# First keys projected ahead of the sketch's turn, third group's factors ahead of turns that wait for loads

## The chip, the cores and the metric

The kernel runs on one core of a Trainium2 chip. The metric is device time in microseconds, the median of several executions; lower is better.

## The reference

Polynomial-sketch attention on 4 batches of 4 heads, 1088 rows of 32, followed by a two-layer network on the rows:

```python
def phi(x):                       # S1, S2: 8 x 32
    a = einsum('rd,bhsd->bhsr', S1, x)
    b = einsum('rd,bhsd->bhsr', S2, x)
    return einsum('bhsi,bhsj->bhsij', a, b).reshape(*x.shape[:-1], 64)

q_p, k_p = phi(q), phi(k)
kv = einsum('bhsf,bhsd->bhfd', k_p, v)
z = sum(k_p, axis=2)
num = einsum('bhsf,bhfd->bhsd', q_p, kv)
den = einsum('bhsf,bhf->bhs', q_p, z)[..., None] + 1e-06
x = (num / den).transpose(0, 2, 1, 3).reshape(4352, 128)
h = x @ w_in                      # 128 x 2048
out = (h - tanh(h)) @ w_out       # 2048 x 128
```

## The kernel before

The 4352 rows are cut into eleven groups (`GROUPS`) of 256 to 512 rows; group 0 to 2 belong to batch 0, group 3 begins batch 1, and group 5 holds the end of batch 1 and the beginning of batch 2. Each batch first needs its keys. Each group needs the factors of its queries, then the numerators, then the rows x, then 16 blocks of the first layer with tanh on ACT, and 16 of the second.

**The planner.** Every instruction, or short run of instructions, is an operation with an engine, an expected cost in ns, a priority and its data dependences (`Program.op`). `Program.listed` places the operations by a list schedule over the expected costs, `schedule` takes the best of six passes, and each engine then carries out its operations in exactly that order. `Program.line(tags)` adds an order between named operations: each comes after the one named before it, also across engines. The change is in such lines alone, so no operation is added or removed by it; the planner runs again on the new order, and the place of every other operation can change with it.

**Names used below.** b is a batch, g a group.
- `pS` (L499), `wkm` (L502), `pSel` (L515), `s2m` (L518): the sketch matrices, turned by PE and masked by DVE. `pSel` writes the PSUM bank that `wkm` reads, so it waits for `wkm`.
- `kTb0`, `kTb1` (L537): DVE's turns of the two parts of a batch's k. `kp00`, `kp01` (L544): PE's projections of the keys of batch 0, in two halves; the other batches have one. `kabb` (L555): DVE's turn of these. `kpsb` (L561): a copy to PSUM. `wkb0`, `wkb2` (L570): products of key factors on DVE; the rest (`wk03` and so on) are made by POOL. `gramb` (L581, PE), `gmb` (L588, DVE), `foldb` (L593, PE), `ub` (L596, DVE): from the key factors to a weight that the queries of the batch need for their denominators.
- `sumsb` (L609), `kvzb` (L617), `turnb` (L620), `ndwb` (L623): the sums over a batch's keys.
- `qTg` (L631): DVE's turn of a group's q. `pg` (L653, PE), `qqg` (L682), `aug` (L685), `dng` (L688, all DVE), `dsg` (L697, PE), `rdg` (L700), `ang` (L704, DVE): factors and the reciprocal denominators. `qpg0`, `qpg1` (L716): products, on DVE and POOL for groups 0, 1 and the first of a batch, on POOL alone for the others. `qpTg0`, `qpTg1` (L723): DVE's turns of these.
- `wg` (L669, PE): the numerators. `xg` (L731): the rows, copied by ACT for groups 0 and 1, by DVE for the others.
- `hg_j` (L792, PE) and `tg_j` (L795, ACT): a block of the first layer and its tanh, over three PSUM banks in turn. L805: the second layer, summed in one bank. The linear part h @ w_out is taken together as one 128x128 matrix (`wtx`, `wcx`, `wp`; its two halves at L772, L773) and added at L784. L812 turns the finished rows into `osb`, and L818 issues the stores.
- L483 and L494 are matmuls on zeros with which the planner fills idle time of PE early in the kernel.

**The loads.** Batch 0 is loaded by ACT's and SP's queues at the start. `lk1`, the first load of batch 1, waits for `qpT01`; v and q of batch 1 follow it in SP's queue. The loads of batch 2 wait for `x2` and those of batch 3 for `x4`; the stores at L818 share this queue.

**The order written by hand.** DVE's first 33 operations stand in one line (L911 to L913). In it `s2m` comes before `kab0`, `qT0` before `kps0`, and after `qpT11` come `kT10` and `kT11`. The factors of group 2 (`qq2` to `an2`) and `qT3` are in no line. PE's first operations stand in the line of L919, with `pSel` right after `pS`.

Of the kernel before, what the change touches and what calls it, by code (L numbers as in the profile page):

```python
# [307 lines left out]
def bass_polysketch_attn__then__act_tanh_shrink_kernel(nc, q, k, v, S1, S2, moe_w_in, moe_w_out, out):  # L308
    P = Program(nc)

    def sb(name, shape, dtype=F32):
        return nc.alloc_sbuf_tensor(name, shape, dtype).ap()
# [21 lines left out]
    s2m = sb("s2m", [128, H, D])  # L334
    wkm = sb("wkm", [128, 2, R, 2])
# [7 lines left out]
    wk = sb("wk", [128, 9, 4, 64])  # L343
# [34 lines left out]
    b = c = at = 0  # L378
    for n0, n1 in GROUPS:
        parts = [(b, c, n0)]  # L380
        c += n0
        if n1:
            assert n1 == n0
            b, c = b + 1, n1
# [3 lines left out]
        if c == CB:  # L388
            b, c = b + 1, 0
# [481 lines left out]
    for g in range(NG):  # L871
# [35 lines left out]
        if g:  # L907
            layers(g)
    P.tags["lq1"].deps.add(P.tags["kT00"])
    P.tags["lk1"].deps.add(P.tags["qpT01"])  # L910
    P.line(["kT00", "wkm", "kT01", "s2m", "kab0", "qT0", "kps0", "gm0", "wk00", "u0", "wk02", "qq0", "au0", "dn0", "qT1",  # L911
            "rd0", "an0_1", "an0_0", "qp00", "qpT00", "qpT01", "qq1", "au1", "dn1", "qT2",
            "rd1", "an1_1", "an1_0", "qp10", "qpT10", "qpT11", "kT10", "kT11"])  # L913
    for g in range(4, NG):
        P.line([f"x{g - 2}", f"qT{g}"])
    for b in range(2, B):
        P.line([f"x{first[b] - 2}", f"kT{b}0", f"kT{b}1"])
    P.line(["x1", "kT10"])
    P.line(["pS", "pSel", "kp00", "kp01", "gram0", "fold0", "p0", "sums00", "ds0", "sums01", "turn0", "p1", "w0"])  # L919
    P.line(["w0", "h0_2", "ds1", "wt0", "w1", "p2"])  # L920
    P.line(["kvz0", "cin0", "ndw0", "cin1", "x0", "t0_0"])
    P.line(["t0_2", "cin2"])
# [32 lines left out]
```

## Time and profile before

| | before |
|---|---|
| median of 3 runs | 108.63 us (107.75 to 108.82) |
| profiled execution | 109.61 us |
| its span | 107.8 us |
| PE busy | 102.2 us (95%), 1287 matmuls |
| ACT busy | 80.5 us (75%) |
| DVE busy | 65.4 us (61%) |
| POOL busy | 33.3 us (31%) |
| granted clock of TensorE | 1.0 |

The span is the part of one execution that the profiler covers; the execution's own time has some 1.8 us around it. In a timeline a row gives its start, its length, the engine, the line of the code, the operation, the tiles, and, in brackets, how long the engine was idle before and what ended that. Instructions of one engine can overlap by the latency of the pipeline, so the distance from one start to the next is often shorter than the length of a row. The ends of matmuls are modelled.

### The profile page before, as it was taken

The page shows a single profiled execution, that of the slowest core. Times are in us where ns is not written, and L with a number is a line of the kernel's source. Part 1 is how long each engine was busy: PE and PEld are TensorE (multiplying, and loading weights), DVE is VectorE, ACT ScalarE, POOL GpSimd, SP SyncE. Part 2 cuts the span into 40 slices and gives each one's busy share as a digit, 9 for nine tenths or more (in the row PEclk, how much of TensorE's full clock was granted, in tenths as well). Part 3 has the DMA queues.
Part 4 walks back from the last instruction along what each step waited for, and adds up shares of the span by engine and source line. Part 5 has one row for each costly group of instructions (what it writes and reads, how often), then busy time and mean ns, then how long its engine had stood idle before and what let it go on. Part 6 is the DMA issues. An engine that isn't in the chain of part 4 may idle for free.

```text
span 107.8 us, 3131 instructions
## 1 busy us (share of the span) xinstructions
PE 102.2 (95%) x1287; PEld 54.0 (50%) x1287; DVE 65.4 (61%) x164; ACT 80.5 (75%) x193; POOL 33.3 (31%) x59
## 2 busy tenths in 40 slices
PE   6999999997899999999999999999999999999990
PEld 4524656582437444535645534454664634545580
DVE  3556987636971859966379359687366657234030
ACT  0004459999476976897797998798698899999960
POOL 6549437006550300781120420088030060030000
PEclk9999999999999999999999999999999999999999
DMA  2998999800089405005895104000410502203223
GB/s 61 323 275 232 368 252 274 233 17 0 9 258 235 178 5 85 0 6 84 274 290 114 23 0 73 6 3 7 72 25 0 91 0 33 43 0 48 43 44 78
DMA packets 23678, 11.21 MB, mean 104 GB/s; under 512 B 17648, under 2 KB 22384, under 8 KB 23664
## 3 DMA queue, kind: packets, MB, share of 16 engines
q1 hardware_dynamic: 20144, 7.44, 29.8%
q10 hardware_dynamic: 3520, 3.57, 11.0%
q8 instruction: 10, 0.16, 0.7%
q14 instruction: 4, 0.03, 0.1%
HBM read 8.78 MB, written 2.23 MB: 102 GB/s over the span
## 4 chain that ended last, share of the span: by engine, by line
PE 64%; DMA 11%; DVE 7%; SPq 7%; ACT 5%; POOL 2%; issue 1%
PE ps L792 21%; PE ps L805 19%; DMA qraw<-in_q_dram 11%; PE ps L483 6%; ACT tt L795 5%; SPq L434 5%; PE ps L669 3%; PE ps L784 3%; PE ps L653 3%; PE ps L544 2%; PE ps L609 2%; PE ps L830 2%; SPq L818 2%; POOL qp L716 2%; DVE qT L631 2%; DVE qpT L723 1%
## 5 line engine op out<-in xcount | busy, mean ns | idle before, releaser
L795 ACT ACTIVATE tt<-ps 128x448 bf16<-128x448 f32 (+3 forms) x176 | 73.9, 525 | 9.5 <-PE ps L792 8.8
L792 PE MATMUL ps<-xT,w_in 128*128 128x448 bf16 (+3 forms) x176 | 56.6, 334 | 0.3
L805 PE MATMUL ps<-tt,w_out 128*128 128x448 bf16 (+3 forms) x160 | 49.9, 336 | 0.0
L792 PEld LDWEIGHTS ps<-xT,w_in 128*128 128x128 bf16 x176 | 16.8, 97 | 23.8 <-ACT tt L795 14.1
L716 POOL TENSOR_TENSOR qp<-an,qq 128x384 f32<-128x384 f32 (+3 forms) x17 | 14.5, 855 | 41.7 <-DVE an L704 40.9
L805 PEld LDWEIGHTS ps<-tt,w_out 128*128 128x128 bf16 x160 | 16.4, 103 | 7.8
L570 POOL TENSOR_TENSOR wk<-kab 128x256 f32<-128x256 f32 (+1 forms) x18 | 12.6, 700 | 17.7 <-DVE kab L555 16.6
L723 DVE STREAM_TRANSPOSE qpT<-qp 128x448 f32<-128x448 f32 (+3 forms) x22 | 12.4, 581 | 5.4 <-POOL qp L716 5.2
L812 DVE STREAM_TRANSPOSE osb<-ps 128x448 f32<-128x448 f32 (+3 forms) x10 | 6.0, 602 | 8.3 <-PE ps L792 4.1
L700 DVE RECIPROCAL ps<-ps 128x28 f32<-128x28 f32 (+3 forms) x11 | 3.4, 313 | 11.0 <-PE ps L697 11.0
L483 PE MATMUL ps<-wz 128*128 128x256 bf16 (+1 forms) x27 | 8.0, 437 | 1.1 <-DVE hmask L460 1.1
L631 DVE STREAM_TRANSPOSE qT<-qraw 128x256 f32<-128x256 f32 (+2 forms) x12 | 6.4, 530 | 3.1 <-DMA qraw<-in_q_dram 3.1
L682 DVE STREAM_TRANSPOSE qq<-ps 128x448 f32<-128x448 f32 (+3 forms) x11 | 6.4, 577 | 2.4 <-PE ps L653 2.3
L617 ACT ACT_TABLE_LOAD x1 | 1.3, 1283 | 8.5 <-DVE ps L561 8.5
L669 PE MATMUL ps<-qpT,ndw 64*32 64x224 f32 (+3 forms) x176 | 6.2, 339 | 0.9 <-DVE qpT L723 0.9
L537 DVE STREAM_TRANSPOSE kT<-kraw 128x576 f32<-128x576 f32 (+1 forms) x8 | 5.6, 721 | 1.1 <-DMA kraw<-in_k_dram 1.1
L731 DVE CAST xT<-ps 128x384 bf16<-128x384 f32 (+3 forms) x9 | 5.5, 606 | 1.1 <-PE ps L669 0.9
L653 PE MATMUL ps<-qT,wq 64*32 64x224 f32 (+3 forms) x176 | 6.1, 334 | 0.0
L570 DVE TENSOR_TENSOR wk<-kab,ps 128x512 f32<-128x512 f32 (+1 forms) x8 | 5.1, 645 | 0.0
L609 PE MATMUL ps<-wk,vx 128*32 128x64 f32 x288 | 5.1, 221 | 0.0
L609 PEld LDWEIGHTS ps<-wk,vx 128*32 128x32 f32 x288 | 4.2, 110 | 1.4 <-issue 1.3
L483 PEld LDWEIGHTS ps<-wz 128*128 128x128 bf16 x27 | 3.0, 130 | 3.7 <-issue 1.7
(74 smaller groups left out, 82.6 us busy)
## 6 DMA issues: line engine op xcount, KB each, us to landing
kraw<-in_k_dram SPq DMA_DIRECT2D x3, 544.0 KB, 4.5
qraw<-in_q_dram SPq DMA_DIRECT2D x3, 544.0 KB, 6.4
vx<-in_v_dram SPq DMA_DIRECT2D x10, 144.0 KB, 4.1
w_in_f<-in_moe_w_in_dram ACTq DMA_DIRECT2D x2, 512.0 KB, 7.5
w_out_f<-in_moe_w_out_dram ACTq DMA_DIRECT2D x2, 512.0 KB, 8.5
out_dram<-osb SPq DMA_DIRECT2D x16, 56.0 KB, 1.9
out_dram<-osb SPq DMA_DIRECT2D x16, 48.0 KB, 1.8
vx<-in_v_dram SPq DMA_DIRECT2D x4, 112.0 KB, 5.0
```

The source lines that it names most:

```text
L483: P.op("tensor", 213 if x < 16 else 221, lambda e, n=1 if x < 16 else 2: e.matmul(ps[:, 3, 0:256 * n], wz[:, 0:128], wz[:, None, :].to_bro ...
L570: P.op(eng, (dve if eng == "vector" else pool)(64 * n), lambda e: e.tensor_tensor(out=wk[:, t0:t1, :, :].rearrange("p t h (i j) -> p (t h) ...
L609: ins = e.matmul(ps[32 * h:32 * h + 32, sbk, 0:64], vx[i][:, h, t, :], wk[:, t, h, :], start=(t == 0), stop=(t == 8), tile_position=(0, 32 ...
L631: P.op("vector", dve(hi - lo), lambda e, i=b % 2, lo=lo, hi=hi: e.transpose(out=qT[i][:, lo:hi], in_=qraw[i][:, lo:hi]), r=[("qraw", b % 2 ...
L653: ins = e.matmul(o, wq[64 * r:64 * r + 64, b, y, :, :].rearrange("p h x -> p (h x)"), src, start=True, stop=True, tile_position=(64 * r, 3 ...
L669: ins = e.matmul(ps[32 * h:32 * h + 32, 2 + u, 0:32 * nh], ndw[i][64 * u:64 * u + 64, 32 * h:32 * h + 32], src[64 * u:64 * u + 64, h // 2, ...
L682: P.op("vector", dve(16 * n), lambda e: e.transpose(out=a[:, 0:n, :].rearrange("p (r m) x -> p r (m x)", r=2), in_=ps[:, pb[0]:pb[1] + 1:p ...
L716: P.op("vector" if dv else "gpsimd", (dve if dv else pool)(32 * m), lambda e, lo=lo, dv=dv: e.tensor_tensor(out=qp[u][:, lo:lo + m, :].rea ...
L723: P.op("vector", dve(32 * m), lambda e, lo=lo: e.transpose(out=qpT[u][:, 32 * lo:32 * (lo + m)], in_=qp[u][:, lo:lo + m, :].rearrange("p n ...
L792: P.op("tensor", pe(n), lambda e, jb=jb, bk=bk: e.matmul(bk[:, 0:n], w_in[:, 128 * jb:128 * jb + 128], xT[:, t0:t0 + n], start=True, stop= ...
L795: P.op("scalar", act(n), lambda e, ts=ts, bk=bk: e.activation(out=tt[:, ts, 0:n], in_=bk[:, 0:n], func=AF.Tanh, scale=-1.0), r=[kb], w=[(" ...
L805: P.op("tensor", pe(n), lambda e, jb=jb, ts=ts: e.matmul(acc[:, 0:n], w_out[:, jb, :], tt[:, ts, 0:n], start=(jb == 0 and not g), stop=(jb ...
```

## The change

The diff changes the lines of order and nothing else:

```diff
-    P.line(["kT00", "wkm", "kT01", "s2m", "kab0", "qT0", "kps0", "gm0", "wk00", "u0", "wk02", "qq0", "au0", "dn0", "qT1",
+    P.line(["kT00", "wkm", "kT01", "kab0", "kps0", "s2m", "gm0", "qT0", "wk00", "u0", "wk02", "qq0", "au0", "dn0", "qT1",
             "rd0", "an0_1", "an0_0", "qp00", "qpT00", "qpT01", "qq1", "au1", "dn1", "qT2",
-            "rd1", "an1_1", "an1_0", "qp10", "qpT10", "qpT11", "kT10", "kT11"])
+            "rd1", "an1_1", "an1_0", "qp10", "qpT10", "qpT11", "qq2", "au2", "dn2", "rd2", "an2", "kT10", "kT11", "qpT21", "qpT20", "qT3"])
     for g in range(4, NG):
         P.line([f"x{g - 2}", f"qT{g}"])
     for b in range(2, B):
         P.line([f"x{first[b] - 2}", f"kT{b}0", f"kT{b}1"])
+        P.line([f"wk{b}0", f"u{b}", f"wk{b}2"])
     P.line(["x1", "kT10"])
-    P.line(["pS", "pSel", "kp00", "kp01", "gram0", "fold0", "p0", "sums00", "ds0", "sums01", "turn0", "p1", "w0"])
+    P.line(["wk10", "u1", "wk12"])
+    P.line(["pS", "kp00", "kp01", "pSel", "gram0", "fold0", "p0", "sums00", "ds0", "sums01", "turn0", "p1", "w0"])
```

In words: on PE the first keys are projected before `pSel`. On DVE `s2m` moves behind `kab0` and `kps0`, and `qT0` behind `gm0`. After `qpT11` the factors of group 2 come first, then the turns of batch 1's keys, then the turns of group 2's products, then `qT3`. For batches 1 to 3, `u` is put between the two key products of DVE.

## The prediction

> **What bounds the kernel now.** I read the page's busy shares and its chain first, then the timelines of PE, DVE and ACT over the first 42 us (nearly all reordered operations lie there), then the chain between 18 and 42 us, and last the loads in SP's queue.
>
> ```profile
> PE 102.2 (95%) x1287; PEld 54.0 (50%) x1287; DVE 65.4 (61%) x164; ACT 80.5 (75%) x193; POOL 33.3 (31%) x59
> PE 64%; DMA 11%; DVE 7%; SPq 7%; ACT 5%; POOL 2%; issue 1%
> ```
>
> PE looks full, but in the first 19 us part of that is filler (L483, L494). The chain is 64% PE, and its 11% of DMA are two waits for q, one before 24 us and one before 39 us. Behind 40 us the chain is PE's matmuls back to back, or ACT's tanhs back to back: those stretches have only throughput, so what is gained ahead of them should be kept to the end.
>
> The start, timelines of PE and DVE:
>
> ```profile
> 4.84 0.79 PE L515 MATMUL ps<-s_raw,sel 16*128 16x128 f32 x2
> 5.56 1.21 PE L544 MATMUL ps<-kT,wkm 64*32 64x288 f32 x16
> 6.71 1.68 PE L483 MATMUL ps<-wz 128*128 128x256 bf16 x4
> 8.31 0.53 PE L581 MATMUL ps<-kab 128*32 128x32 f32 x18
> ...
> 6.88 0.78 DVE L555 STREAM_TRANSPOSE kab<-ps 128x576 f32<-128x576 f32 x1 [0.92 <-PE ps L544]
> 7.59 0.40 DVE L631 STREAM_TRANSPOSE qT<-qraw 128x256 f32<-128x256 f32 x1
> 7.91 0.27 DVE L561 COPY ps<-kab 128x128 f32<-128x128 f32 x1
> 8.88 0.19 DVE L588 TENSOR_TENSOR gm<-ps,bmask 128x32 f32<-128x32 f32 x1 [0.70 <-PE ps L581]
> 8.99 0.68 DVE L570 TENSOR_TENSOR wk<-kab,ps 128x512 f32<-128x512 f32 x1
> 9.58 0.18 DVE L596 TENSOR_REDUCE wq<-ps 128x16 f32<-128x32 f32 x1
> ```
>
> See that pSel (L515) stands ahead of the key projections kp00 and kp01 (L544); that kab0 follows these at once; that gram0 (L581) starts when the four fillers are through, not when kab0 ends (7.66); and that qT0 (L631) lies in DVE's wait for gram0.
>
> The middle, timelines of DVE, PE and ACT, then SP and DVE again:
>
> ```profile
> 20.18 0.74 DVE L537 STREAM_TRANSPOSE kT<-kraw 128x576 f32<-128x576 f32 x1
> 20.98 0.70 DVE L537 STREAM_TRANSPOSE kT<-kraw 128x512 f32<-128x512 f32 x1
> 21.60 0.24 DVE L688 TENSOR_REDUCE dn<-au 128x24 f32<-128x120 f32 x1
> 23.61 0.65 DVE L631 STREAM_TRANSPOSE qT<-qraw 128x448 f32<-128x448 f32 x1 [1.77 <-DMA qraw<-in_q_dram]
> 24.18 0.28 DVE L700 RECIPROCAL ps<-ps 128x24 f32<-128x24 f32 x1
> 24.50 0.25 DVE L704 TENSOR_TENSOR an<-qq,ps 128x96 f32<-128x96 f32 x1
> 26.64 0.58 DVE L723 STREAM_TRANSPOSE qpT<-qp 128x384 f32<-128x384 f32 x1 [0.17 <-POOL qp L716]
> 27.14 0.74 DVE L555 STREAM_TRANSPOSE kab<-ps 128x576 f32<-128x576 f32 x1
> ...
> 27.27 0.56 PE L669 MATMUL ps<-qpT,ndw 64*32 64x192 f32 x16 [0.85 <-DVE qpT L723]
> 28.65 2.72 ACT L795 ACTIVATE tt<-ps 128x448 bf16<-128x448 f32 x6 [1.37 <-PE ps L792]
> ...
> 33.46 0.44 SPq L441 DMA_DIRECT2D qraw<-in_q_dram  x1
> 38.81 0.45 DVE L631 STREAM_TRANSPOSE qT<-qraw 128x256 f32<-128x256 f32 x1 [1.29 <-DMA qraw<-in_q_dram]
> ```
>
> The product for rd2 (ds2) was done by 22.6 us, but DVE stood at qT3, which waited 1.77 us for the second batch's q. Behind it came rd2, an2, both POOL products, both turns qpT2, and w2 (L669): PE stood still for 0.85 us and ACT for 1.37.
>
> **The change, part by part.** The profiled execution took 109.61 us, its span 107.8; the median of the runs is 108.63, that is 0.98 below it. I work out a difference and take it from each.
>
> *pSel behind kp01.* Both follow wkm, so kp00 can take pSel's place at 4.91 in the chain. kT00 ends at 4.43. kp01 needs kT01, which ends at 5.12; kp00 takes about half of the 1.14, so it isn't held. The chain has pSel from 4.91 to 5.63: kab0 comes 0.72 earlier, at 6.16.
>
> *pSel ahead of gram0.* It keeps its 0.72, now in the gap that the fillers took (chain: 1.61 for four). The code plans fillers at 213 and 221 ns and pSel at 300, so it displaces one or two. With three left, one short (0.23) and two long (0.43 each): 0.72 + 1.09 = 1.81, gram0 at about 6.05 + 1.81 = 7.86 against 8.38 in the chain, 0.52 earlier. With two, 0.9 earlier; with all four, nothing. I take 0.5.
>
> *s2m behind kps0* costs 0.29, inside the 0.70 that DVE waited for gram0. Without that cover it is 0.29 on the path. *qT0 behind gm0* loses that cover: it now stands between gm0 and wk00, u0, with 0.32 (from its start to the next one's, 7.59 to 7.91). So u0 and p0 come 0.5 - 0.32 = about 0.2 earlier; bounds 0.6 earlier (two fillers) and 0.3 later (four).
>
> The clock of the array is a price here that before doesn't show under another order. The long fillers stand 0.43 us apart at 7 us, and the chain has two of them in 0.43 at 9.54: the rate doubles about 9.4 us. I leave that moment alone; if it came after p0 and ds0, these would take up to 0.5 more, which is the upper bound. The Trainium skill (TensorE: Matmul & The Clock Gate, Part 1: The HAM clock gate) has the half rate end after some 3.4 us of sustained activity, in a free-running window, and so would speak against thinning out fillers; the trace, cold from 1.05 to about 9.4 us, differs from that count. By that page the sum would lose the 0.2 again at worst.
>
> *The loads' queue.* lk1 waits for qpT01, which follows p0: lk1, four of v and the second batch's q on SP shift by the same 0.2, and nothing is added to a queue. Their landing (23.6) is then no longer ahead of rd2.
>
> *qq2, au2, dn2, rd2, an2 in a row.* Without kT10 in between, dn2 starts about 20.48 (qq to au 0.49, au to dn 0.27, from group 0's rows) instead of 21.60. dn1 to rd1 took 0.98 from start to start, so rd2 starts about 21.44 and an2 at 21.76, against 24.50: 2.7 earlier. The wait for ds2, some 0.7, now shows on DVE; behind it are kT10, kT11, both qpT2, qT3. kT10 and kT11 (1.4) fit into the time of POOL's two products (0.33 after an2, then 2 x 0.93): they end by 23.4, and the second product by 23.9. Thus qpT20 starts at 23.9, w2 about 24.5, against 27.27. qT3 starts at 24.4, after its data (23.6): no wait, and its user p3 (30.67) has time.
>
> *The keys of batch 1.* kp1 waited for an2 anyway (bank 0; 24.81 behind an2's end); now it waits for kT11, 23.4: 1.4 earlier. kab1 then needs only DVE: about 24.5 to 25 against 27.14.
>
> *wk, u, wk12 for three batches.* u1 stood behind both wk and osb0 (0.66 + 0.44); it comes ahead of these. But if fold is late, DVE stands there and what is behind it, osb0 and x, waits. Batch 1's fold ended 0.46 after gm (28.76 to 29.22 by the chain), batch 2's 0.66; wk takes 0.6. I take nothing; bounds 0.4 gained, 0.6 lost for each of three batches.
>
> *What it is worth.* The last wait in this stage is ACT's for h. Of the 1.37 at 28.65, w2 and gram1 themselves (0.5 + 0.3 on PE) leave perhaps 0.3: 1.1 gained, bounds 0.9 and 1.4. The next wait of ACT, 0.81 before 32.18, is lin, p3 and output matmuls ahead of h; some of it dissolves as p3 moves: 0.3, bounds 0 and 0.8. At 38.81 qT5 waited 1.29 for the third batch's q, holding osb1; ACT lost 0.57 there and PE 0.24. Those loads start when x2 is done, some 2 us earlier, though four output issues wait for osb0 in the same queue. The rest moves 1.4, so about half of the wait goes: 0.3, bounds 0 and 0.5. Sum: 0.2 + 1.1 + 0.3 + 0.3 = 1.9. The profiled execution would take 107.7, the median 106.7; I write 106.8, since the first 0.2 is the weakest term.
>
> **The rivals.**
> A. *The gain is absorbed.* ACT's six tanhs take 2.72 from 28.65 whatever w2 does, and 0.76 of ACT's waits come from the sums' 1.14 on PE, which remain. If p3, kp1, gram1 and sums1 crowd into 23 to 30 us, only half of the 1.1 is kept and the other terms fall away: 0.5 less, 108.1. For it: PE has 0.65 + 0.3 + 0.5 + 1.1 of such work there. Against: this work isn't new, and PE stood.
> B. *Slower: u ahead of wk12 stops DVE.* If PE has h and lin queued ahead of fold, DVE stands with osb and x behind it. u followed gm by 1.48 in batch 1 and by 1.04 in batch 2 while DVE did other work; standing instead, 1.5 + 1.0 + 1.0 = 3.5 lost against 1.9 gained: 110.2. It decides once fold ends over 0.7 behind gm. Against: 0.46 and 0.66 are the traced figures.
> C. *More.* Two fillers only, and all upper bounds: 0.6 + 1.4 + 0.8 + 0.5 = 3.3: 105.3.
> D. *The wait only moves.* If the second batch's q lands over 1 us later than 23.6, qT3 again holds kab1 and x2: 108.6. Against: the loads are no fewer and start no later.
>
> **How the numbers follow.** Forecast 0.48 (its own range 105.9 to 107.6), A 0.18, B 0.22, C 0.08, D 0.04. Faster by over 1% (about what a measurement of this kernel can tell) is the forecast and C: 0.56; A and D are within: 0.22; B is slower: 0.22. The range reaches from C to most of B, which need not come to all three batches: 105.3 to 109.7.
>
> **What would show it.** Right: kab0 near 6.2; an2 near 21.8 with no DMA wait ahead of rd2; w2 near 24.6; no 1.37 of ACT ahead of the second group's tanhs; PE after 40 us the same but earlier by 1.7 to 2. Wrong: gram0 still at 8.3; ds2 behind the product of the weights (23.06), which would put an2 and then kT10 behind 24; DVE waiting for fold with osb behind it; new ACT waits behind 40 us.

## The result and the profile after

Over 21 executions of each, the changed kernel takes 0.9892 [0.9859, 0.9924] of the time of the kernel before: by this ratio it is 1.1% faster, about 1.2 us. Its median is 108.64 us (106.96 to 112.46), against 108.97 (107.75 to 109.82). This ratio and those below leave out executions over 1.5% above the fastest of their kernel (11 of 21 for the changed kernel, 6 of 21 for the one before, 8 of 12 for e1 further down), and over all of them the median fell by only 0.3%, as did the mean (109.01 to 108.68). The profiled execution took 107.36 us with a span of 105.6, against 109.61 and 107.8. The profiles are thus 2.25 us apart, a good deal more than the ratio: the one of before took 0.64 longer than its kernel's median, and the one of the changed kernel 1.28 less.

The page of the changed kernel, busy times and then the chain that ended last, by engine:

```profile
PE 101.1 (96%) x1285; PEld 54.0 (51%) x1288; DVE 65.9 (62%) x164; ACT 80.3 (76%) x193; POOL 33.3 (32%) x59
PE 88%; ACT 9%; DVE 0%; issue 0%
```

The work is the same. What changed is the chain: the 11% of DMA are gone, and so are the shares of DVE, SP and POOL. The chain now runs almost entirely through PE.

The start, timelines of PE and DVE of the changed kernel, to be read beside the first 10 us shown for before:

```profile
4.75 1.57 PE L544 MATMUL ps<-kT,wkm 64*32 64x288 f32 x16
6.25 0.61 PE L515 MATMUL ps<-s_raw,sel 16*128 16x128 f32 x2
...
8.35 1.03 PE L483 MATMUL ps<-wz 128*128 128x512 bf16 x4
9.31 0.45 PE L653 MATMUL ps<-qT,wq 64*32 64x128 f32 x16
...
6.39 0.78 DVE L555 STREAM_TRANSPOSE kab<-ps 128x576 f32<-128x576 f32 x1 [1.31 <-PE ps L544]
8.90 0.18 DVE L596 TENSOR_REDUCE wq<-ps 128x16 f32<-128x32 f32 x1
```

The key projections (L544) stand ahead of pSel (L515), and kab0 starts at 6.39 instead of 6.88. u0 (L596) comes at 8.90 instead of 9.58. On PE, four fillers (L483) lie between the product that u0 reads and p0 (L653).

The middle, timelines of DVE, PE and ACT of the changed kernel:

```profile
21.15 0.32 DVE L700 RECIPROCAL ps<-ps 128x24 f32<-128x24 f32 x1 [0.81 <-PE ps L697]
21.50 0.25 DVE L704 TENSOR_TENSOR an<-qq,ps 128x96 f32<-128x96 f32 x1
...
23.65 0.58 DVE L723 STREAM_TRANSPOSE qpT<-qp 128x384 f32<-128x384 f32 x1 [0.15 <-POOL qp L716]
24.15 0.60 DVE L631 STREAM_TRANSPOSE qT<-qraw 128x448 f32<-128x448 f32 x1
...
25.89 0.56 PE L669 MATMUL ps<-qpT,ndw 64*32 64x192 f32 x16
...
27.08 2.73 ACT L795 ACTIVATE tt<-ps 128x448 bf16<-128x448 f32 x6 [0.22 <-PE ps L792]
30.73 0.54 ACT L795 ACTIVATE tt<-ps 128x448 bf16<-128x448 f32 x1 [0.93 <-PE ps L792]
...
36.78 0.45 DVE L631 STREAM_TRANSPOSE qT<-qraw 128x256 f32<-128x256 f32 x1 [1.07 <-DMA qraw<-in_q_dram]
```

rd2 (L700) waits for PE instead of a transfer. an2 stands at 21.50 (24.50 before), and qT3 (L631, 24.15) finds its data there. ACT's wait of 1.37 ahead of the six tanhs has become 0.22; its next wait has become 0.93 (0.81 before); qT5's wait for the third batch's q has become 1.07 (1.29 before).

**Three stretches.** Executions differ in their start, so I cut each span at two events that every profile has: the start of w1 (L669, the numerators of group 1) and the first tanh of group 2 (L795, 128x384). The labels are those of the experiments further down.

| kernel | to w1 | w1 to group 2's tanh | qT3 waits for q | from there to the end | span |
|---|---|---|---|---|---|
| before | 18.62 | 15.72 | 1.77 | 73.46 | 107.8 |
| start part alone (e1) | 19.56 | 15.81 | 1.86 | 73.13 | 108.5 |
| u lines alone (e3) | 18.77 | 15.89 | 1.22 | 72.94 | 107.6 |
| start, short fillers (e9) | 20.11 | 14.75 | 0.81 | 72.94 | 107.8 |
| before, warmed (e5) | 27.95 | 14.71 | 0.75 | 72.94 | 115.6 |
| start, warmed (e7) | 29.75 | 14.49 | 0.17 | 72.96 | 117.2 |
| middle part alone (e2) | 18.84 | 14.30 | none | 73.16 | 106.3 |
| whole change | 18.10 | 14.42 | none | 73.08 | 105.6 |
| whole change again (e4) | 18.06 | 14.43 | none | 73.81 | 106.3 |
| whole change, warmed (e6) | 28.60 | 14.43 | none | 72.97 | 116.0 |
| whole change and qT5 (e12) | 18.79 | 14.30 | none | 72.71 | 105.8 |

With the middle part the second column is 14.3 to 14.4 in every profile, and qT3 finds its data. Without it the column goes with qT3's wait: it is 15.7 to 15.9 in before, e1 and e3, but only 14.5 to 14.8 in e9, e5 and e7, where q of batch 1 landed 3.4 to 4.0 us after the start of w1 and not 5.0 to 5.2. DVE in e9, and then in e7, whose line numbers are one and two higher:

```profile
24.13 0.65 DVE L632 STREAM_TRANSPOSE qT<-qraw 128x448 f32<-128x448 f32 x1 [0.81 <-DMA qraw<-in_q_dram]
```

```profile
33.13 0.65 DVE L633 STREAM_TRANSPOSE qT<-qraw 128x448 f32<-128x448 f32 x1 [0.17 <-DMA qraw<-in_q_dram]
```

So the middle part is worth about what that load is late: 1.3 to 1.6 us of this stretch where qT3 waited 1.2 us or more, and 0.1 to 0.5 where it waited 0.8 or less.

### The profile page after: what moved, and what is told of

It reads as the page before. It is cut to its first block, busy times and chain, and to the rows that moved or that the text cites. A ratio compares the mean times of both kernels' runs of the same rounds, so it can differ in the third digit from the quotient of the medians.

```text
span 105.6 us, 3129 instructions
## 1 busy us (share of the span) xinstructions
PE 101.1 (96%) x1285; PEld 54.0 (51%) x1288; DVE 65.9 (62%) x164; ACT 80.3 (76%) x193; POOL 33.3 (32%) x59
## 4 chain that ended last, share of the span: by engine, by line
PE 88%; ACT 9%; DVE 0%; issue 0%
PE ps L792 28%; PE ps L805 24%; ACT tt L795 8%; PE ps L483 6%; PE ps L669 5%; PE ps L609 4%; PE ps L653 4%; PE ps L784 3%; PE ps L544 3%; PE ps L830 2%; PE ps L697 2%; PE ps L494 1%; PE ps L581 1%; PE ps L768 1%; PE ps L754 1%; PE ps L593 1%
## 5 line engine op out<-in xcount | busy, mean ns | idle before, releaser
L795 ACT ACTIVATE tt<-ps 128x448 bf16<-128x448 f32 (+3 forms) x176 | 73.7, 527 | 8.0 <-PE ps L792 7.2
L792 PE MATMUL ps<-xT,w_in 128*128 128x448 bf16 (+3 forms) x174 | 55.9, 333 | 0.4
L805 PE MATMUL ps<-tt,w_out 128*128 128x448 bf16 (+3 forms) x159 | 49.4, 336 | 0.1
L716 POOL TENSOR_TENSOR qp<-an,qq 128x384 f32<-128x384 f32 (+3 forms) x17 | 14.5, 854 | 39.1 <-DVE an L704 38.3
L700 DVE RECIPROCAL ps<-ps 128x28 f32<-128x28 f32 (+3 forms) x11 | 3.5, 315 | 10.4 <-PE ps L697 10.4
L483 PE MATMUL ps<-wz 128*128 128x256 bf16 (+1 forms) x28 | 7.3, 398 | 1.1 <-DVE hmask L460 1.1
L631 DVE STREAM_TRANSPOSE qT<-qraw 128x256 f32<-128x256 f32 (+2 forms) x12 | 6.4, 531 | 1.2 <-DMA qraw<-in_q_dram 1.1
L669 PE MATMUL ps<-qpT,ndw 64*32 64x224 f32 (+3 forms) x176 | 6.2, 339 | 0.0
L653 PE MATMUL ps<-qT,wq 64*32 64x224 f32 (+3 forms) x176 | 6.1, 333 | 0.0
L555 DVE STREAM_TRANSPOSE kab<-ps 128x576 f32<-128x576 f32 x4 | 3.1, 783 | 2.3 <-PE ps L544 2.3
```

The source lines that it names most:

```text
L483: P.op("tensor", 213 if x < 16 else 221, lambda e, n=1 if x < 16 else 2: e.matmul(ps[:, 3, 0:256 * n], wz[:, 0:128], wz[:, None, :].to_bro ...
L631: P.op("vector", dve(hi - lo), lambda e, i=b % 2, lo=lo, hi=hi: e.transpose(out=qT[i][:, lo:hi], in_=qraw[i][:, lo:hi]), r=[("qraw", b % 2 ...
L653: ins = e.matmul(o, wq[64 * r:64 * r + 64, b, y, :, :].rearrange("p h x -> p (h x)"), src, start=True, stop=True, tile_position=(64 * r, 3 ...
L669: ins = e.matmul(ps[32 * h:32 * h + 32, 2 + u, 0:32 * nh], ndw[i][64 * u:64 * u + 64, 32 * h:32 * h + 32], src[64 * u:64 * u + 64, h // 2, ...
L716: P.op("vector" if dv else "gpsimd", (dve if dv else pool)(32 * m), lambda e, lo=lo, dv=dv: e.tensor_tensor(out=qp[u][:, lo:lo + m, :].rea ...
L792: P.op("tensor", pe(n), lambda e, jb=jb, bk=bk: e.matmul(bk[:, 0:n], w_in[:, 128 * jb:128 * jb + 128], xT[:, t0:t0 + n], start=True, stop= ...
```

## The experiments

The theory was that the middle part (qT3 out of the way of rd2 and an2) carries nearly all of the gain, the start some tenths, and the u lines nothing. The rivals were that the start carries it, and that the gain is an accident of the profiled pair.

**e1, e2, e3: one part alone; e4: the whole change again.** e1 has the two edits of the start and nothing else:

```diff
-"kT00","wkm","kT01","s2m","kab0","qT0","kps0","gm0","wk00"
+"kT00","wkm","kT01","kab0","kps0","s2m","gm0","qT0","wk00"
-"pS","pSel","kp00","kp01","gram0"
+"pS","kp00","kp01","pSel","gram0"
```

> Only the start is changed: pSel behind kp01 on PE, s2m behind kps0 and qT0 behind gm0 on DVE; everything from qpT11 on keeps the order of before. Theory (each part has its own gain, most of it in the middle): u0 and p0 0.2 us earlier, 0 to 0.5 us in the time, so 108.3 to 108.9 beside a before of 108.8. Rival 1 (the start carries the gain, since the two profiles differ by 0.53 us at w1 already and the start's clock differs): 1 us or more, below 107.9. Rival 2 (the first profiles differ in when the array's clock doubles, 9.4 against 6.5 us, and with the same moment the start gains nothing, since qT0 now stands on DVE's path): 0, or 0.2 slower.

e2 has the longer end of DVE's line alone:

```diff
-"qpT11", "kT10", "kT11"])
+"qpT11", "qq2", "au2", "dn2", "rd2", "an2", "kT10", "kT11", "qpT21", "qpT20", "qT3"])
```

> Only the line behind qpT11 is changed (qq2, au2, dn2, rd2, an2, then kT10, kT11, qpT21, qpT20, qT3). Theory: an2 3 us earlier than before relative to w1, ACT's wait of 1.37 before the second group's next tanhs shrinks to about 0.2, and the time falls by 1.2 to 1.6 us, to about 107.4. Rival (the start carries the gain): under 0.5 us. It should show the same place of w2, about 7.8 us behind w1, if PE's queue and not DVE sets it.

e3 has the lines of `wk`, `u`, `wk` alone:

```diff
+        P.line([f"wk{b}0", f"u{b}", f"wk{b}2"])
+    P.line(["wk10", "u1", "wk12"])
```

> Only the lines wk, u, wk2 for batches 1 to 3 are added. Theory: p3, p5 and the like come some 0.1 to 0.5 us earlier and nothing waits for them: 0 to 0.3 us gained, 108.5 to 108.8. Rival (DVE stands for fold): slower by 0.5 us or more, with a wait of DVE ahead of u in the trace.

e4 is the changed kernel as it is.

> The changed kernel unaltered, for a second profile and more times on the chip of the other three. If the clock of the array doubles at another moment in this profile than 6.5 us, its w1 should move with it: about 0.2 us for each us of the moment, and the time with w1. Theory of separate parts: its gain is the sum of the other three, 1.3 to 2.2 us. Rival (clock): the gain lies between 0.8 and 1.4 and the spread from execution to execution is as large as that.

| | ratio to before | median | mean of all executions |
|---|---|---|---|
| before | | 109.01 | 109.00 |
| e1, start | 0.9952 [0.9899, 1.0005] | 109.88 | 109.70 |
| e2, middle | 0.9890 [0.9853, 0.9928] | 108.10 | 108.41 |
| e3, u lines | 1.0010 [0.9966, 1.0054] | 108.89 | 108.90 |
| e4, whole | 0.9899 [0.9858, 0.9939] | 107.92 | 107.88 |

The middle alone has the ratio of the whole, though its 0.9 by the median is less than the 1.2 to 1.6 expected of it. e4 repeats the ratio of the change with a median 1.1 below that of before; the 1.3 to 2.2 that was expected if the parts add up was not reached, and 1.1 lies in the range given to its rival. The u lines show no effect. The start alone has an interval that reaches across 1, and a median 0.9 above that of before. Two timelines bear on it. First PE in e1, the start alone, and behind it PE in before:

```profile
9.39 1.56 PE L483 MATMUL ps<-wz 128*128 128x512 bf16 x4
10.88 0.45 PE L653 MATMUL ps<-qT,wq 64*32 64x128 f32 x16
```

```profile
9.37 0.59 PE L483 MATMUL ps<-wz 128*128 128x512 bf16 x2
9.91 0.45 PE L653 MATMUL ps<-qT,wq 64*32 64x128 f32 x16
```

The profiled execution of e1 took 110.26 us, 0.4 above its median. In e1 u0 ended at 9.91, but p0 stands behind four fillers and starts at 10.88, 0.97 later. In the profile of before two fillers stood there (9.37 to 9.96), and p0 started at 9.91, 0.15 behind u0. The planner counts 221 ns for each. In e1 the first three of the four took 1.34, so the array was at half rate for most of them; in the changed kernel's profile all four took 1.03, and p0 lost only 0.23.

Now POOL and DVE in e2, which has the start of before:

```profile
6.87 3.36 POOL L570 TENSOR_TENSOR wk<-kab 128x512 f32<-128x512 f32 x3 [0.18 <-DVE kab L555]
...
9.33 0.98 DVE L685 TENSOR_TENSOR au<-qq 128x64 f32<-128x64 f32 x1
15.73 0.58 DVE L631 STREAM_TRANSPOSE qT<-qraw 128x384 f32<-128x384 f32 x1 [1.18 <-DMA qraw<-in_q_dram]
```

Here the array reached its full rate at about 5.0 us, and u0 came at 7.96: 1.62 ahead of before's profile with the same order. Yet w1 came at 18.84, no earlier than before's 18.62. au0 took 0.98 (0.24 before) while POOL was at its key products, and qT2, which stands in DVE ahead of rd1, waited 1.18 for the first batch's third piece of q. Of an early start, these two take back the gain.

**e5, e6, e7: the start with the array warmed ahead of it.** To take the moment of the doubling out of the comparison, 32 matmuls on zeros run first, and the first load of each queue waits for them. e5 is so made from before, e6 from the changed kernel, e7 from e1. (In the diff the body of the added operation is left out. One constant goes with it: the time from which the planner holds fillers back moves from 3700 to 13300 ns.)

```diff
+    pre = P.op("tensor", 300 * 32, ...)   # 32 matmuls of 512 columns on zeros
+    o.deps.add(P.tags["pre"])             # for the first load of each queue
```

> The order of before behind 32 more matmuls on zeros (512 columns) that PE does first; the first load of each queue waits for them, so that the array's clock has doubled before any real work and everything else is shifted. The time is that of before plus the prefix (8 to 13 us, by how long it is cold), less what the cold start cost: 116 to 121 us. Theory (the moment of the clock sets much of the spread): w0 stands at the same distance behind the first k's landing in every profile, and the executions agree better than the 2 to 3 us of before. Rival (the spread is the loads'): the spread stays. Only the differences to the next two kernels are read.

> The changed kernel behind the same prefix. Theory (the middle gives 1.3 and the rest little): 1.2 to 1.5 us below e5. If the start adds its share with a warm array: 1.6 to 2.0 below. Rival (the gain came from the moment of the clock): under 0.5 us.

> Only the start's part of the change behind the same prefix. Theory (the fillers cost the start what it lost on a cold array: planned at 221 ns, they took 430): with a warm array the start is worth -0.2 to +0.4 us against e5, no longer a loss of 0.9 in the median as on the cold one. Rival (qT0 behind gm0 is the loss): 0.3 us slower than e5, warm or cold.

Measured as ratios to before, the added stretch included: 1.0786 [1.0723, 1.0850], 1.0816 [1.0760, 1.0872] and 1.0818 [1.0751, 1.0886]. The three can't be told apart, and the design failed. The first load was issued at 10.06, 10.74 and 10.09, so the added stretch itself varied, and PE then stood for 1.4 to 1.7 us until the first load landed. In e5 the granted clock falls to 6 and 7 tenths in two slices, in e7 to 5, 5 and 7 in three, while e6 has 9 throughout. The rate was thus not held. Nor could the middle part show much here: qT3 waits only 0.75 in e5, and the stretch behind w1 is 14.71 there and 14.43 in e6. But e6 and e7, which have the same order at the start, became a pair of a warm and a cold array. PE in e7, where L485 is the L483 of the others:

```profile
18.85 1.89 PE L485 MATMUL ps<-wz 128*128 128x512 bf16 x4
```

The four fillers took 1.89, and p0 began at 20.67, 1.30 behind u0's end. In e6 they took 1.03, and p0 began 0.23 behind u0. That is the loss of e1 once more.

**e9, e10: the four fillers shortened.** If the fillers were the loss, four of 64 columns, in the same order and with the same planned cost, should free it. e9 is e1 with that edit, e10 the changed kernel with it.

```diff
+    ... c=64 if 19 <= x < 23 else 256 ...    # columns of the fillers between fold0 and p0
```

> The start's part alone (as e1), with the four fillers that the planner put between fold0 and p0 cut from 512 to 64 columns; the order of everything is that of e1. Theory (these fillers, planned at 221 ns and taking 430 on a cold array, hold p0 behind u0 by up to 1.2 us): p0 follows u0 by 0.2 to 0.3 us in the profile whatever the clock does, and the median falls from e1's 109.9 to about 108.6 beside a before of 109.0. Rival (qT0 behind gm0 is the loss): no change against e1. Risk: with less work the array may stay cold longer.

> The changed kernel with the same four fillers cut to 64 columns. Theory: its best times stay near 107.0, but the upper half of its executions (108.6 to 110.5) comes down by up to 1 us; median 107.5 to 108.0. Rival (the loads set the spread): spread and median as the changed kernel's, 107 to 110.5, 108.6.

e9: 0.9998 [0.9954, 1.0042], median 109.64; e10: 0.9937 [0.9900, 0.9974], median 108.38 (before 109.25). Neither gained on its parent, where medians of 108.6 and of 107.5 to 108.0 were expected. In e9, PE, one line number higher:

```profile
10.08 0.68 PE L654 MATMUL ps<-qT,wq 64*32 64x128 f32 x16 [0.17 <-DVE wq L597]
```

p0 does follow u0 at once (u0 from 9.84 to 10.02). But the array stayed at half rate until about 13.9 us: p0 took 0.68 where it had taken 0.45, the sums behind it 1.72 where 0.99, rd0 waited 0.84 for PE, and w1 came at 20.11, later than in any other kernel without the added stretch. In e10 the array was warm at about 5.1 us, and qT2 waited 1.51 for q. So my account of the start was only half of it: the fillers ahead of p0 cost, but taking them away bought nothing; in e9 the array stayed slow, and in e10 q wasn't there. The rival to e9, that qT0 behind gm0 is the loss, forecast this result and is in part borne out: from gm0's start to u0's it is 1.04 us in the changed kernel, e1 and e9, and 0.70 in before and e2. These 0.34 are lost whatever the fillers do.

**e8, e11, e12: qT5 out of the way of osb1.** The changed kernel repeats, near 38 us, what it mends near 24: qT5 waits for a transfer, with osb1 behind it. One more line puts the second half of qT5, the one with batch 2's rows, behind x3: e8 on e2, e11 on e10, e12 on the changed kernel.

```diff
     P.line(["x1", "kT10"])
+    P.line(["x3", "qT5b"])
```

> The middle's part alone, with one more line: qT5b, the turn that waits for the third batch's q, comes after x3 instead of ahead of osb1. In six profiles DVE stood there for 0.96 to 1.90 us. Theory (same fix as qT3's): ACT's wait near 38 us falls from 0.24 to 1.18 to about 0.2, and the time by 0.3 to 0.9 us against e2: 107.3 to 107.8. Rival (osb1's delay is hidden): no change against e2.

> e10 with qT5b behind x3, as in e8. Theory (the two are separate): 0.2 to 0.9 us below e10, by how late the third batch's q lands; the fastest version here, about 107.3 in the median. Rival (osb1's delay is hidden): the same as e10.

> The changed kernel, its fillers whole, with qT5b behind x3 as in e8 and e11. Theory (qT5b's wait for the third batch's q is what is left of the waits of this kind, and the short fillers of e11 give nothing): ACT's wait near 38 us is 0.16, and the time is 0.2 to 0.9 us below the changed kernel's, a ratio of 0.980 to 0.987 to before. Rival (e11's gain came from the short fillers): 0.989 as the changed kernel.

| | ratio to before | median | its parent's ratio |
|---|---|---|---|
| e8 | 0.9878 [0.9821, 0.9936] | 108.00 | 0.9890 (e2) |
| e11 | 0.9837 [0.9775, 0.9898] | 107.85 | 0.9937 [0.9900, 0.9974] (e10) |
| e12 | 0.9849 [0.9806, 0.9893] | 107.39 (before 109.10) | 0.9892 and 0.9899 |

e8 was expected 0.3 to 0.9 us below e2; by the ratios it is 0.1% below, which its interval can't tell from nothing. DVE in e12, and then in e4, the changed kernel without that line:

```profile
37.07 0.65 DVE L812 STREAM_TRANSPOSE osb<-ps 128x448 f32<-128x448 f32 x1 [0.79 <-PE ps L805]
```

```profile
37.56 0.45 DVE L631 STREAM_TRANSPOSE qT<-qraw 128x256 f32<-128x256 f32 x1 [1.90 <-DMA qraw<-in_q_dram]
```

In e12 osb1 waits only for PE, and ACT's wait near 39 us is 0.16. In e4 qT5 holds osb1 for 1.90, and ACT's wait there is 1.18. The last stretch of the table is 72.6 to 72.7 in e8, e11 and e12, and 72.9 to 73.8 in the eight comparable profiles without the line. e12 has the lowest median of all kernels run here. That it beats the changed kernel rests on e11 against e10, whose intervals part by a hair (0.9898 and 0.9900), and on the profiles; e12's own interval overlaps the changed kernel's.

## Why the prediction was right, and where its sum was off

**The time.** The forecast was 106.8, with 105.9 to 107.6 as its own range. By the ratio the changed kernel takes 107.5 where the one before takes 108.63, inside that range. The median over all 21 executions is 108.64, outside it and close to the rivals A (108.1) and D (108.6), so the time alone doesn't decide between these; the traces do.

**The middle, predicted 1.1: right in mechanism, and in size for these profiles.** an2 was forecast at 21.76 and came at 21.50; the wait for ds2 on DVE was to be about 0.7 and was 0.81; qT3 was to find its data and did; ACT's wait was to fall from 1.37 to 0.3 and fell to 0.22. The stretch from w1 to group 2's tanh shrank by 1.3 to 1.4 against the profile of before, in whichever kernel the part was put. Two things here were luck. w1 came 0.52 earlier than in before, which hides that an2 came 3.40 behind w1 and not 3.14 (21.76 less 18.62). And the size was taken from one profile in which q landed late; against e9, e5 and e7 the same part is worth 0.1 to 0.5.

**Right end by a wrong step: w2.** qpT20 was forecast at 23.9 and came at 23.65, so DVE was in time. But w2 (L669) came at 25.89, not 24.5: it wasn't idle PE that it met, but PE's queue, in which the planner had put the weights' product (L768, 22.84), six blocks of h and kp1 (24.40, forecast 23.4) ahead of it. It cost nothing, since those blocks of h kept ACT fed. That ACT's wait is the measure, and not w2's start, was the part of the step that held.

**The wait of 0.81, predicted 0.3 gained: wrong.** It is 0.93 in the changed kernel. I had let "some of it dissolve" as p3 moves; nothing did.

**The wait near 38 us, predicted 0.3 gained: not sure.** qT5's wait was 1.29 before and 1.07 after, but 0.96 and 0.98 in e1 and e3, and 1.90 in e4. q of batch 2 was issued 1.4 us earlier than before (32.05 against 33.46), not 2, behind four stores and three loads of v, and q landed 4.7 us after issue in one execution of the changed kernel and 5.7 in the other. That spread is larger than the term. What the wait is worth shows in the profiles in which it is moved away (e8, e11, e12): about half a microsecond in the last stretch.

**The start, predicted 0.2: no gain that can be shown.** qT0's price was right (0.34 for 0.32). Three things were mis-sized. kab0 came 0.49 earlier and not 0.72: I wrote that kp01 "isn't held" by kT01, but the two projections took 1.57 from start to end, against 1.21, and in e6 the second waits 0.16 for DVE's turn. In e1, with the array at half rate as in before, gram0 came 0.18 earlier (8.13 against 8.31) and not 0.52, and u0 0.16 later (9.74 against 9.58). The fillers were counted ahead of gram0 only; qT0 behind gm0 widened the gap ahead of p0, and the planner put four there in place of two. And behind both stand q's landing and POOL's products, which took back the earlier start in e2. The bound of 0.3 later that I gave was too small: in e1's profile p0 came 0.97 later than in that of before (10.88 against 9.91).

**The clock of the array**, which I left alone, is one thing in which the two first profiles differ besides the order. From the spacing of the fillers (0.43 or 0.215 us), the rate doubled between 8.8 and 9.4 us in the profile of before and at about 6.5 in that of the changed kernel, so that the 0.5 us by which the latter reaches w1 earlier is no evidence for the order. In e2, whose first 10 us have the order of before, it came at about 5.0. The Trainium skill (TensorE: Matmul & The Clock Gate, Part 1: The HAM clock gate) has the full rate come after some 3.4 us of sustained activity, counted in a free-running window, and calls the cold stretch variable from run to run for that reason; the variation agrees with these profiles, the length doesn't, since PE is in work from 1.05 us on. Only where matmuls of 512 columns ran back to back from 1.05 us on was it near that: 3.9 us after this in e5 and e7, 5.3 in e6.

**The rivals.** A (absorbed, 108.1) and D (the wait only moves) fell in the traces, with ACT's 0.22 and with qT3 not waiting. B (u stops DVE) fell in e3: the ratio is 1.0010, and in the changed kernel u1 follows gm1 by 1.39 with other work of DVE between, so DVE did not stand there. C (more) was not reached. The sum of 1.9 against about 1.2 by the ratio is too large by the start's 0.2 and by the two waits of 0.3, of which no gain was shown.

**Open.** What decides when the rate doubles (3.7 to 13.9 us over eleven profiles) was not settled, and e5 to e7 could not hold it. Nor was it settled why the landing of the same load differs: q of batch 1 took 4.9 us from issue to landing in e7 and 8.2 in e12. How much the whole change is worth over all executions is open too: in its first 21 the mean fell by 0.3 us, in the 6 of e4 by 1.1. The changed kernel's times spread by 5.5 us over those 21, those of before by 2.1; but before spreads by 3.4 over the 29 executions beside e1 to e4, as e1 does over 12, so the runs don't tie the spread to the start part. A start with fewer fillers planned at their cold length was not tried.

## What to carry to other kernels

In an engine that works in a fixed order, put a turn that waits for a transfer behind the work that needs no transfer, and then look for the next place with the same pattern: here the first was worth 1.1% by the ratio of e2, and the second between 0.1% (e8) and 1.0% (e11). Before you size such a step, look in several profiles how late the transfer comes: the step gains about that wait, and in e7 there was hardly any. Fillers that keep an array busy are work in the queue like any other: planned at their fast length, they block the path when the array is slow. Before a gain at the start of a kernel is credited to an edit, align several profiles at a later event that all have; here kernels with the same order at the start reached w1 at 18.62 to 19.21 (before, e2, e3, e8) and at 18.06 to 18.79 (the changed kernel, e4, e12), where the edit was to gain 0.2.

## What the runs showed that I had not expected

- The array's rate doubled anywhere between 3.7 and 13.9 us into the span: three fillers of 256 columns took 0.50 at 3.98 us in e8 and 0.82 at 4.09 in before, and in e9 p0 still took 0.68 at 10.08. The row of the granted clock shows 9 throughout in those pages that have it; in the views only the spacing of equal matmuls tells. The same row does show the drop in e5 and e7, after PE had stood for 1.70 and 1.40 us; in e6, after 1.41, there was none.
- A product on DVE with both inputs in SBUF took 0.98 us beside POOL's key products, against 0.23 in e1, where these were done. In e2 it ended at 10.31 and POOL's products at 10.23; in the changed kernel it took 0.34 and ended at 10.69, and POOL's ended at 10.61. The Trainium skill (SBUF — State Buffer, Who interferes with whom) describes such a pair as taking turns at a shared port, the later one blocked until the other's instruction ends; these rows agree.
